# Assembling fp64 weights by clamp, shift, sign merge and integer addition; attention reads in two column tiles; state loads on two queues

## The chip, the cores and the metric

One core of a Trainium2 chip. The metric is the device time of one execution in microseconds (us), lower is better. Engines: PE = TensorE, PEld = its weight loads, DVE = VectorE, ACT = ScalarE, POOL = GpSimd, SP = SyncE. The profiler also records the clock that PE was granted, as a share of full speed; "half clock" below is 0.50 of it.

## The reference

A block-recurrent cross attention, then a gated MLP. The weights come as fp64, the rest as fp32.

```python
# x: (8, 8, 512, 64), state: (8, 8, 32, 64); w_in: (512, 2048), w_out: (2048, 512)
s1 = softmax(x @ state.T / 8);  xread = s1 @ state        # tokens read the states
s2 = softmax(state @ x.T / 8);  sread = s2 @ x            # states read the tokens ("reads")
h = reshape(concat([xread, sread])) @ w_in                # (4352, 512) @ (512, 2048)
out = (h * cos(h)) @ w_out
```

## The kernel before

The batch elements follow each other. For each, the attention is cut into small pieces that stand between the big matmuls of the MLP: `hidden(t)` (weights times attention, into `h`), a gate on ACT and DVE, and `output(t)`. There are 16 slots `t` per batch element. In the first one the weights, which come as pairs of 32-bit words, are also turned into fp32, one chunk per slot, `conv = 3 + t`. All small pieces share one PSUM tile, `at`.

```python
def states():                         # both halves, before the scores
    for half in range(2):
        ...                           # 4 transposes into at[:, half]
        nc.scalar.activation(stS[:, dst], src, func=ACTF.Copy, scale=scale)
        nc.vector.tensor_scalar(stT[:, dst], src, 1.0 / TWO_PI, None, op0=ALU.mult)

def convert1(i):                      # cut: raw, dst, hi, e
    nc.vector.tensor_scalar(e, hi, 0x7FF00000, None, op0=ALU.bitwise_and)       # exponent
    nc.vector.tensor_scalar(dst.bitcast(I32), hi, 0xFFFFF, None, op0=ALU.bitwise_and)
    nc.scalar.activation(e, e, func=ACTF.Relu, bias=ebias, scale=8.0)
    nc.scalar.activation(raw_lo_f32, raw_lo_u32, func=ACTF.Copy, scale=2.0**-52, bias=1.0)
def convert2(i):
    nc.vector.scalar_tensor_tensor(out=e, in0=hi, scalar=-2**31, in1=e, ...)    # sign
    nc.vector.scalar_tensor_tensor(out=dst, in0=dst, scalar=2.0**-20, in1=raw_lo_f32, ...)
def convert3(i):
    nc.vector.tensor_tensor(dst, dst, e.bitcast(F32), op=ALU.mult)

def reads(self, j):
    for c in range(NC):               # 4 matmuls of 256 columns (each is two on PE)
        nc.tensor.matmul(out=at[:, 0, cols], lhsT=self.a2T[:, j, c, :], rhs=..., ...)

for t in tiles(b):                    # one slot
    hidden(t)
    if conv and t.f: convert1(conv + 1); convert2(conv)
    gate(t); gate2(t)                 # ACT copy, DVE
    if conv: convert3(conv)           # cut: the first slot does two chunks
    gate3(t)                          # ACT: Abs, Sin
    go(); ...; output(...)            # go(): one small piece
    gate4(t)                          # DVE
    go()
```

Of the kernel before, what the change touches and what calls it, by code (L numbers as in the profile page):

```python
# [9 lines left out]
F32 = mybir.dt.float32  # L10
I32 = mybir.dt.int32
U32 = mybir.dt.uint32
ALU = mybir.AluOpType
ACTF = mybir.ActivationFunctionType
# [5 lines left out]
TWO_PI = 2.0 * math.pi  # L20
# [3 lines left out]
def kernel(  # L24
# [8 lines left out]
    nc = tc.nc  # L33

    B, H, S, D = x.shape
    Ns = state.shape[2]
    Dm, Dff = moe_w_in.shape
    P = 128
    NK = Dm // P
    NF = Dff // P  # L40
    NC = S // P
    T = S + Ns
    WC = 512
    scale = 1.0 / math.sqrt(D)

    consts = ctx.enter_context(tc.tile_pool(name="consts", bufs=1))
    wraw = ctx.enter_context(tc.tile_pool(name="wraw", bufs=3))
    cvt = ctx.enter_context(tc.tile_pool(name="cvt", bufs=2))
# [14 lines left out]

    halfpi = consts.tile([P, 1], F32)
    nc.vector.memset(halfpi, math.pi / 2.0)
    ebias = consts.tile([P, 1], F32)
    nc.vector.memset(ebias, -896.0 * 2.0 ** 23)




    st = consts.tile([P, B, 2 * D], F32)
    stT = consts.tile([P, B, P], F32)
    stS = consts.tile([P, B, P], F32)
    ident = consts.tile([P, P], F32)
# [4 lines left out]
    def load_x(b):  # L80

        x_b = xin.tile([P, NC, H, D], F32, name="x_b")
        src = x[b].rearrange("h (c p) d -> c p h d", p=P)
        for c in range(NC):
            nc.sync.dma_start(out=x_b[:, c], in_=src[c])
        x_t[b] = x_b
# [2 lines left out]
    st_src = state.rearrange("b (k j) n d -> j k n b d", j=2)  # L89
    for k in range(NK):  # L90
        for j in range(2):
            nc.scalar.dma_start(
                out=st[Ns * k:Ns * k + Ns, :, D * j:D * j + D],
                in_=st_src[j, k])


    at = aps.tile([P, 2, S], F32, name="at")

    def states():
        for half in range(2):  # L100
            for i in range(4):
                nc.tensor.transpose(out=at[:, half, P * i:P * i + P],
                                    in_=st[:, 4 * half + i, :], identity=ident)
            dst = slice(4 * half, 4 * half + 4)
            src = at[:, half].rearrange("p (b m) -> p b m", b=4)
            nc.scalar.activation(stS[:, dst], src, func=ACTF.Copy, scale=scale)
            nc.vector.tensor_scalar(stT[:, dst], src, 1.0 / TWO_PI, None,
                                    op0=ALU.mult)

    w_in = consts.tile([P, NK, Dff], F32)  # L110
    w_out = consts.tile([P, NF, Dm], F32)
# [8 lines left out]
    def in_load(c0, c1, k):  # L120
        return w_in[:, k:k + 2, c0:c1], w_in_src[:, k:k + 2, c0:c1]

    def out_load(f):
# [3 lines left out]
    loads = [in_load(HC * i, HC * i + HC, k) for i in range(2)  # L127
             for k in range(0, NK, 2)]
# [10 lines left out]
    def fetch(n):  # L139
        nonlocal n_fetched  # L140
        while n_fetched < min(n, len(loads)):
            dst, src = loads[n_fetched]
            if f64:
                raw = wraw.tile([P, 2, WC, 2], I32, name="raw")
                raw = raw[:, :, 0:dst.shape[2]]
                nc.sync.dma_start(out=raw.rearrange("p m f w -> p m (f w)"),
                                  in_=src.bitcast(I32))
                raws[n_fetched] = raw
            else:
                nc.sync.dma_start(out=dst, in_=src)  # L150
            n_fetched += 1

    half = {}
# [1 line left out]



    def convert1(i):
        if not f64 or i >= len(loads):
            return  # L160
        raw = raws.pop(i)
        dst = loads[i][0]
        hi = raw[:, :, :, 1]
        e = cvt.tile([P, 2, WC], I32, name="e")[:, :, 0:dst.shape[2]]
        nc.vector.tensor_scalar(e, hi, 0x7FF00000, None, op0=ALU.bitwise_and)  # L165
        nc.vector.tensor_scalar(dst.bitcast(I32), hi, 0xFFFFF, None,
                                op0=ALU.bitwise_and)
        nc.scalar.activation(e, e, func=ACTF.Relu, bias=ebias, scale=8.0)  # L168
        nc.scalar.activation(raw.bitcast(F32)[:, :, :, 0],
                             raw.bitcast(U32)[:, :, :, 0], func=ACTF.Copy,  # L170
                             scale=2.0 ** -52, bias=1.0)
        half[i] = raw, e

    def convert2(i):
        if i not in half:
            return
        raw, e = half[i]
        dst = loads[i][0]
        nc.vector.scalar_tensor_tensor(out=e, in0=raw[:, :, :, 1],  # L179
                                       scalar=-2 ** 31, in1=e,  # L180
                                       op0=ALU.bitwise_and, op1=ALU.bitwise_or)
        nc.vector.scalar_tensor_tensor(out=dst, in0=dst.bitcast(I32),  # L182
                                       scalar=2.0 ** -20,
                                       in1=raw.bitcast(F32)[:, :, :, 0],
                                       op0=ALU.mult, op1=ALU.add)

    def convert3(i):
        if i not in half:
            return
        raw, e = half.pop(i)  # L190
        dst = loads[i][0]
        nc.vector.tensor_tensor(dst, dst, e.bitcast(F32), op=ALU.mult)
        fetch(i + 4)


# [4 lines left out]
    class Attention:  # L200
# [30 lines left out]
        def all_tokens(self):  # L231

            xp = [ops.tile([P, Dm], F32, name="o") for k in range(NK)]
            for c in range(NC):
                for k in range(NK):
                    self.turn_x(k, c, xp[k])
            for k in range(NK):
                if k % 2 == 0:
                    nc.scalar.copy(self.xT[:, k], xp[k])
                else:  # L240
                    nc.vector.tensor_copy(self.xT[:, k], xp[k])
# [73 lines left out]



        def reads(self, j):
            cols = slice(NK * D * j, NK * D * j + NK * D)
            for c in range(NC):  # L320
                nc.tensor.matmul(  # L321
                    out=at[:, 0, cols], lhsT=self.a2T[:, j, c, :],
                    rhs=self.x_b[:, c].rearrange("p (k j) d -> p j k d",
                                                 j=2)[:, j],
                    start=(c == 0), stop=(c == NC - 1))

        def keep(self):
            self.inverse(self.i2)
            src = at[:, 0].rearrange("p (j k d) -> p j k d", j=2, k=NK)
            for k in range(NK):  # L330
                rows = slice(Ns * k, Ns * k + Ns)
                nc.vector.tensor_tensor(
                    self.sr[rows], src[rows, :, k, :],
                    self.i2[rows].unsqueeze(2).to_broadcast([Ns, 2, D]),
                    op=ALU.mult)

# [67 lines left out]
    def gate3(t):  # L404
        nc.scalar.activation(t.q, t.q, func=ACTF.Abs)  # L405
        nc.scalar.activation(t.q, t.q, func=ACTF.Sin, bias=halfpi,  # L406
                             scale=-TWO_PI)
# [53 lines left out]
    fetch(3)  # L461
    a0 = attn[0] = Attention(0)
    a0.all_tokens()
    states()
    a0.scores()
    convert1(0)
    a0.max1()
    a0.spread1()
    a0.shift()
    a0.exp1()  # L470
    convert2(0)
    convert3(0)
    a0.sums()
    convert1(1)
    a0.spread1()
# [3 lines left out]
    a0.first_products(HC)  # L479
    a0.max2()  # L480
    a0.exp2()
    load_x(1)
    convert1(2)
    convert1(3)


# [13 lines left out]
    for b in range(B + 1):  # L500
        work = parts(b + 1) if b + 1 < B else []
        if b == 1:
            work = P1[1:] + work
        n_slots, slot, n_done = 2 * NF, 0, 0

        def go():
            nonlocal n_done, slot
            if b == 0:
                for part in slots0[slot]:
                    part()  # L510
            slot += 1
            want = (len(work) * slot + n_slots - 1) // n_slots
            while n_done < want and b > 0:
                work[n_done]()
                n_done += 1

        for t in tiles(b):
            if t.f == NF // 2 and b + 2 < B:
                load_x(b + 2)
            conv = 3 + t.f if b == 0 else None  # L520
            hidden(t)
            if conv and t.f:
                convert1(conv + 1)
                convert2(conv)
            gate(t)
            gate2(t)
            if conv:
                if t.f == 0:
                    convert2(conv - 1)
                    convert3(conv - 1)  # L530
                    convert2(conv)
                convert3(conv)
            gate3(t)
            go()
            line.append(t)
            if len(line) > 4:
                output(line.pop(0))
            gate4(t)
            if conv and t.f == 0:
                convert1(conv + 1)  # L540
            go()
    for t in line:
        output(t)

# [1 line left out]
_INS = ['x', 'state', 'moe_w_in', 'moe_w_out']  # L546
_OUTS = [((4352, 512), 'float32')]
# [25 lines left out]
```

## Time and profile before

| | before |
|---|---|
| median of the first runs | 892.11 us (891.3 to 893.52) |
| profiled execution | 891.4 us |
| PE, DVE, ACT busy | 93%, 39%, 47% of it |

These shares are averages over three stages with different limits. The lines shown in the prediction below separate them: a chain of latencies to 35 us, the conversion to 147 us, and then PE without a pause. The busy time of one engine in each stretch is what to read.

How much a piece between two big matmuls costs is read from the chain: the next matmul's start, and whether the next ones are longer than usual.

### The profile page before, as it was taken

How to read it: one execution, taken by the hardware profiler on the slowest of the kernel's cores; microseconds unless marked ns; L12 is line 12 of the kernel's file. 1: busy time of each engine (PE TensorE's matmuls, PEld its weight loads, DVE VectorE, ACT ScalarE, POOL GpSimd, SP SyncE). 2: the span in 40 equal slices, each digit the busy share in tenths (PEclk: the TensorE clock that was granted, in tenths of full speed). 3: DMA queues.
4: the chain of work that ended last, by engine and by line, in shares of the span. 5: the costliest groups of instructions: out<-in, count | busy, mean ns of one | idle time of the engine just before them, and what ended most of it. 6: DMA issues, size and time to landing. Idle time of an engine off the chain costs nothing.

```text
span 891.4 us, 7090 instructions
## 1 busy us (share of the span) xinstructions
PE 833.2 (93%) x2720; PEld 382.2 (43%) x2720; DVE 346.3 (39%) x504; ACT 417.8 (47%) x648; POOL 0.7 (0%) x6
## 2 busy tenths in 40 slices
PE   3369968999999999999999999999999999999997
PEld 2025324344444453445344544444344534445664
DVE  1888986234313431352224422442235222222121
ACT  2476574446344634463446434553446344433332
POOL 0000000000000000000000000000000000000000
PEclk9979989999999999999999999999999999999999
DMA  6555620030001200030003000300010000000100
GB/s 141 143 173 179 188 96 1 1 95 1 0 1 57 38 0 1 1 95 1 0 1 95 0 1 0 95 0 1 1 47 1 0 1 24 24 0 1 47 1 24
DMA packets 45377, 35.05 MB, mean 39 GB/s; under 512 B 36384, under 2 KB 36384, under 8 KB 45344
## 3 DMA queue, kind: packets, MB, share of 16 engines
q1 hardware_dynamic: 43168, 34.08, 13.5%
q10 hardware_dynamic: 2176, 0.52, 0.3%
q8 instruction: 21, 0.34, 0.2%
q14 instruction: 12, 0.10, 0.0%
HBM read 25.69 MB, written 8.91 MB: 39 GB/s over the span
## 4 chain that ended last, share of the span: by engine, by line
PE 85%; DVE 7%; ACT 4%; DMA 2%; issue 1%; ACTq 0%; DVEq 0%
PE o L421 49%; PE h L391 26%; PE at L248 4%; PE at L321 3%; DMA st<-in_state_dram 1%; PE at L222 1%; DVE e L179 1%; DVE q L400 1%; PE at L310 1%; ACT q L406 1%; DVE w_out L182 1%; ACT q L405 1%; DVE e L165 1%; DVE w_in L182 1%; ACT e L168 1%
## 5 line engine op out<-in xcount | busy, mean ns | idle before, releaser
L421 PE MATMUL o<-w_out,g 128*128 128x512 f32 x1088 | 492.3, 595 | 0.0
L421 PEld LDWEIGHTS o<-w_out,g 128*128 128x128 f32 x1088 | 203.4, 190 | 244.5 <-issue 240.9
L391 PE MATMUL h<-aT,sw 128*128 128x512 f32 x512 | 249.6, 611 | 2.5 <-ACT sw L353 2.0
L400 DVE SCALAR_TENSOR_TENSOR q<-q,h 128x512 f32<-128x512 f32 (+1 forms) x144 | 94.4, 656 | 338.3 <-ACT q L397 338.2
L397 ACT ACTIVATE q<-h 128x512 f32<-128x512 f32 (+1 forms) x144 | 82.4, 573 | 239.5 <-PE h L391 239.5
L411 DVE TENSOR_TENSOR g<-h,q 128x512 f32<-128x512 f32 (+1 forms) x144 | 95.3, 662 | 161.9 <-ACT q L406 161.9
L391 PEld LDWEIGHTS h<-aT,sw 128*128 128x128 f32 x512 | 95.8, 194 | 121.0 <-issue 107.2
L405 ACT ACTIVATE q<-q 128x512 f32<-128x512 f32 (+1 forms) x144 | 87.3, 606 | 114.5 <-DVE q L400 114.5
L406 ACT ACTIVATE q<-q,halfpi 128x512 f32<-128x512 f32 (+1 forms) x144 | 100.5, 698 | 4.5
L248 PE MATMUL at<-w_in,stT 64*32 64x512 f32 (+1 forms) x512 | 36.8, 616 | 13.7 <-ACT z L287 6.6
L353 ACT COPY sw<-at 128x1024 f32<-128x1024 f32 (+1 forms) x32 | 31.6, 987 | 24.9 <-PE at L248 24.9
L321 PE MATMUL at<-x_b,a2T 128*128 128x256 f32 x128 | 30.6, 382 | 0.0
L391 PE MATMUL h<-sT,w_in 128*128 128x256 f32 x128 | 30.2, 379 | 0.0
L321 PEld LDWEIGHTS at<-x_b,a2T 128*128 128x128 f32 x128 | 24.7, 193 | 10.8 <-issue 8.0
L168 ACT ACTIVATE e<-e,ebias 128x1024 int32<-128x1024 int32 (+1 forms) x18 | 19.0, 1054 | 22.0 <-DVE e L165 22.0
L427 ACT ACTIVATE ot<-o 128x512 f32<-128x512 f32 x34 | 19.3, 591 | 20.8 <-DMA out_dram<-ot 14.1
L391 PEld LDWEIGHTS h<-sT,w_in 128*128 128x128 f32 x128 | 24.3, 190 | 10.1 <-issue 5.3
L222 PEld LDWEIGHTS at<-ident,x_b 128*128 128x128 f32 x112 | 14.7, 148 | 21.8 <-issue 12.6
L222 PE MATMUL at<-ident,x_b 128*128 128x128 f32 x112 | 18.0, 286 | 6.2 <-ACT xT L229 6.2
L248 PEld LDWEIGHTS at<-w_in,stT 64*32 64x32 f32 x512 | 6.1, 106 | 39.8 <-issue 17.6
L229 ACT COPY xT<-at 128x512 f32<-128x512 f32 x28 | 16.0, 573 | 10.1 <-PE at L222 10.1
L179 DVE SCALAR_TENSOR_TENSOR e<-raw,e 128x1024 int32<-128x1024 int32 (+1 forms) x18 | 19.8, 1100 | 0.0
(52 smaller groups left out, 272.5 us busy)
## 6 DMA issues: line engine op xcount, KB each, us to landing
x_b<-in_x_dram SPq DMA_DIRECT2D x32, 256.0 KB, 4.7
raw<-in_moe_w_out_dram SPq DMA_DIRECT2D x8, 1024.0 KB, 4.9
out_dram<-ot SPq DMA_DIRECT2D x32, 256.0 KB, 2.1
raw<-in_moe_w_in_dram SPq DMA_DIRECT2D x6, 1024.0 KB, 5.3
raw<-in_moe_w_in_dram SPq DMA_DIRECT2D x4, 512.0 KB, 6.9
st<-in_state_dram ACTq DMA_DIRECT2D x8, 64.0 KB, 4.9
out_dram<-ot SPq DMA_DIRECT2D x8, 64.0 KB, 1.7
```

Source lines behind the costliest of these rows:

```text
L179: nc.vector.scalar_tensor_tensor(out=e, in0=raw[:, :, :, 1], scalar=-2 ** 31, in1=e, op0=ALU.bitwise_and, op1=ALU.bitwise_or)
L222: nc.tensor.transpose(out=out[:, P * c:P * c + P], in_=self.x_b[:, c, 2 * k:2 * k + 2, :], identity=ident)
L248: nc.tensor.matmul(out=(to[j] if to else at[:, j])[Ns * k:Ns * k + Ns, 0:n], lhsT=w[D * j:D * j + D, self.b, Ns * k:Ns * k + Ns], rhs=r(sl ...
L321: nc.tensor.matmul(out=at[:, 0, cols], lhsT=self.a2T[:, j, c, :], rhs=self.x_b[:, c].rearrange("p (k j) d -> p j k d", j=2)[:, j], start=( ...
L353: nc.scalar.copy(sw_of[self.b, nt][:, :, c0:c1], at[:, :, 0:c1 - c0])
L391: nc.tensor.matmul(out=t.hp, lhsT=t.lhs(i), rhs=t.rhs(i), start=(i == 0), stop=(i == t.kn - 1))
L397: nc.scalar.activation(t.q, t.hp, func=ACTF.Copy, bias=MAGIC)
L400: nc.vector.scalar_tensor_tensor(out=t.q, in0=t.q, scalar=MAGIC, in1=t.hp, op0=ALU.subtract, op1=ALU.subtract)
L405: nc.scalar.activation(t.q, t.q, func=ACTF.Abs)
L406: nc.scalar.activation(t.q, t.q, func=ACTF.Sin, bias=halfpi, scale=-TWO_PI)
L411: nc.vector.tensor_tensor(t.g[:, 0:t.n], t.hp, t.q, op=ALU.mult)
L421: nc.tensor.matmul(out=acc[i], lhsT=t.g[:, P * i:P * i + P], rhs=w_out[:, t.f, :], start=(t.f == 0), stop=(t.f == NF - 1))
```

## The change

The intent is a conversion with four DVE operations per chunk instead of five, reads that use the array as two tiles of 64 columns side by side, and an earlier start. ACT now begins the conversion (`convert0`), and its two passes stand between the gate and `gate3`. The diff is cut.

```diff
-            nc.scalar.dma_start(
+            queue = nc.scalar if j == 0 else nc.gpsimd
+            queue.dma_start(
...
-    def convert1(i):   # two ANDs on DVE, Relu and Copy on ACT
+    def convert0(i):
+        nc.scalar.activation(dst, raw.bitcast(F32)[:, :, :, 1], func=ACTF.Abs)
+        nc.scalar.activation(e, raw.bitcast(U32)[:, :, :, 0], func=ACTF.Copy,
+                             scale=2.0 ** -51, bias=2.0)
+    def convert1(i):
+        nc.vector.tensor_scalar(dst, dst, 2.0 ** -15, None, op0=ALU.max)
+        nc.vector.tensor_scalar(dst.bitcast(I32), dst.bitcast(I32), 3, None,
+                                op0=ALU.logical_shift_left)
     def convert2(i):
+        nc.vector.scalar_tensor_tensor(out=dst, in0=raw[:, :, :, 1],
+                                       scalar=-2 ** 31, in1=dst,
+                                       op0=ALU.bitwise_and, op1=ALU.bitwise_xor)
     def convert3(i):
-        nc.vector.tensor_tensor(dst, dst, e.bitcast(F32), op=ALU.mult)
+        nc.vector.tensor_tensor(dst, dst, e.bitcast(I32), op=ALU.add)
...
-            for c in range(NC):          # x transposes of the first batch element
-                for k in range(NK):
+            for k in range(NK):
+                for c in range(NC):
                     self.turn_x(k, c, xp[k])
...
         def reads(self, j):
+                for k in range(0, NK, 2):
+                    rows = slice(Ns * k, Ns * k + 2 * Ns)
+                    nc.tensor.matmul(
+                        out=at[rows, 0, cols], lhsT=self.a2T[:, j, c, rows],
+                        rhs=x_c[:, j, k:k + 2], start=(c == 0),
+                        stop=(c == NC - 1), tile_position=(0, Ns * k))
...
-    states()
+    states(0)
     a0.scores()
...
     a0.exp2()
+    convert0(2)
+    convert1(2)
+    states(1)
...
             if conv and t.f:
-                convert1(conv + 1)
+                convert1(conv)
                 convert2(conv)
             gate(t)
             gate2(t)
...
                 convert3(conv)
+                convert0(conv + 1)
             gate3(t)
```

More of the change, by code (lines that the diff above doesn't have):

```diff
@@ L65 @@
     nc.vector.memset(halfpi, math.pi / 2.0)
-    ebias = consts.tile([P, 1], F32)
-    nc.vector.memset(ebias, -896.0 * 2.0 ** 23)
     st = consts.tile([P, B, 2 * D], F32)
@@ L97, with states @@
     at = aps.tile([P, 2, S], F32, name="at")
-    def states():
-        for half in range(2):
-            for i in range(4):
-                nc.tensor.transpose(out=at[:, half, P * i:P * i + P],
-                                    in_=st[:, 4 * half + i, :], identity=ident)
-            dst = slice(4 * half, 4 * half + 4)
-            src = at[:, half].rearrange("p (b m) -> p b m", b=4)
-            nc.scalar.activation(stS[:, dst], src, func=ACTF.Copy, scale=scale)
-            nc.vector.tensor_scalar(stT[:, dst], src, 1.0 / TWO_PI, None,
-                                    op0=ALU.mult)
+    def states(half):
+        for i in range(4):
+            nc.tensor.transpose(out=at[:, half, P * i:P * i + P],
+                                in_=st[:, 4 * half + i, :], identity=ident)
+        dst = slice(4 * half, 4 * half + 4)
+        src = at[:, half].rearrange("p (b m) -> p b m", b=4)
+        nc.scalar.activation(stS[:, dst], src, func=ACTF.Copy, scale=scale)
+        nc.vector.tensor_scalar(stT[:, dst], src, 1.0 / TWO_PI, None,
+                                op0=ALU.mult)
     w_in = consts.tile([P, NK, Dff], F32)
@@ L162, in convert1 @@
         dst = loads[i][0]
-        hi = raw[:, :, :, 1]
-        e = cvt.tile([P, 2, WC], I32, name="e")[:, :, 0:dst.shape[2]]
-        nc.vector.tensor_scalar(e, hi, 0x7FF00000, None, op0=ALU.bitwise_and)
-        nc.vector.tensor_scalar(dst.bitcast(I32), hi, 0xFFFFF, None,
-                                op0=ALU.bitwise_and)
-        nc.scalar.activation(e, e, func=ACTF.Relu, bias=ebias, scale=8.0)
-        nc.scalar.activation(raw.bitcast(F32)[:, :, :, 0],
-                             raw.bitcast(U32)[:, :, :, 0], func=ACTF.Copy,
-                             scale=2.0 ** -52, bias=1.0)
-        half[i] = raw, e
+        n = dst.shape[2]
+        e = cvt.tile([P, 2 * WC], F32, name="e")[:, 0:2 * n]
+        e = e.rearrange("p (m f) -> p m f", m=2)
+        nc.scalar.activation(dst, raw.bitcast(F32)[:, :, :, 1], func=ACTF.Abs)
+        nc.scalar.activation(e, raw.bitcast(U32)[:, :, :, 0], func=ACTF.Copy,
+                             scale=2.0 ** -51, bias=2.0)
+        half[i] = raw, e
+    def convert1(i):
+        if i not in half:
+            return
+        dst = loads[i][0]
+        nc.vector.tensor_scalar(dst, dst, 2.0 ** -15, None, op0=ALU.max)
+        nc.vector.tensor_scalar(dst.bitcast(I32), dst.bitcast(I32), 3, None,
+                                op0=ALU.logical_shift_left)
     def convert2(i):
@@ L177, in convert2 @@
         raw, e = half[i]
-        dst = loads[i][0]
-        nc.vector.scalar_tensor_tensor(out=e, in0=raw[:, :, :, 1],
-                                       scalar=-2 ** 31, in1=e,
-                                       op0=ALU.bitwise_and, op1=ALU.bitwise_or)
-        nc.vector.scalar_tensor_tensor(out=dst, in0=dst.bitcast(I32),
-                                       scalar=2.0 ** -20,
-                                       in1=raw.bitcast(F32)[:, :, :, 0],
-                                       op0=ALU.mult, op1=ALU.add)
+        dst = loads[i][0].bitcast(I32)
+        nc.vector.scalar_tensor_tensor(out=dst, in0=raw[:, :, :, 1],
+                                       scalar=-2 ** 31, in1=dst,
+                                       op0=ALU.bitwise_and,
+                                       op1=ALU.bitwise_xor)
     def convert3(i):
@@ L190, in convert3 @@
         raw, e = half.pop(i)
-        dst = loads[i][0]
-        nc.vector.tensor_tensor(dst, dst, e.bitcast(F32), op=ALU.mult)
+        dst = loads[i][0].bitcast(I32)
+        nc.vector.tensor_tensor(dst, dst, e.bitcast(I32), op=ALU.add)
         fetch(i + 4)
@@ L233, in all_tokens @@
             xp = [ops.tile([P, Dm], F32, name="o") for k in range(NK)]
-            for c in range(NC):
-                for k in range(NK):
+            for k in range(NK):
+                for c in range(NC):
                     self.turn_x(k, c, xp[k])
-            for k in range(NK):
                 if k % 2 == 0:
@@ L318, in reads @@
         def reads(self, j):
-            cols = slice(NK * D * j, NK * D * j + NK * D)
+            cols = slice(2 * D * j, 2 * D * j + 2 * D)
             for c in range(NC):
-                nc.tensor.matmul(
-                    out=at[:, 0, cols], lhsT=self.a2T[:, j, c, :],
-                    rhs=self.x_b[:, c].rearrange("p (k j) d -> p j k d",
-                                                 j=2)[:, j],
-                    start=(c == 0), stop=(c == NC - 1))
+                x_c = self.x_b[:, c].rearrange("p (k j) d -> p j k d", j=2)
+                for k in range(0, NK, 2):
[4 more added lines that the diff above has]
+                        stop=(c == NC - 1), tile_position=(0, Ns * k))
         def keep(self):
             self.inverse(self.i2)
-            src = at[:, 0].rearrange("p (j k d) -> p j k d", j=2, k=NK)
+            src = at[:, 0, 0:4 * D].rearrange("p (j k d) -> p j k d", j=2,
+                                              k=2)
             for k in range(NK):
@@ L332, in keep @@
                 nc.vector.tensor_tensor(
-                    self.sr[rows], src[rows, :, k, :],
+                    self.sr[rows], src[rows, :, k % 2, :],
                     self.i2[rows].unsqueeze(2).to_broadcast([Ns, 2, D]),
@@ L463 @@
     a0.all_tokens()
-    states()
+    states(0)
     a0.scores()
+    convert0(0)
     convert1(0)
@@ L472 @@
     convert3(0)
+    convert0(1)
     a0.sums()
@@ L481 @@
     a0.exp2()
+    convert0(2)
+    convert1(2)
+    states(1)
     load_x(1)
-    convert1(2)
+    convert0(3)
     convert1(3)
@@ L538 @@
             gate4(t)
-            if conv and t.f == 0:
-                convert1(conv + 1)
             go()
```

## The prediction

> **What bounds the kernel now.** I read the engine totals first, then busy time by stage, then the chain of work that ended last, then the groups by shape, then single stretches of the timeline.
>
> The stage table splits the run in three (columns: stretch, its length, busy us and instruction counts of PE, PEld, DVE, ACT, POOL, then granted clock, DMA share, GB/s):
>
> ```profile
> 0.00:35.00 35.00, 11.21 (x57) 5.41 (x58) 16.44 (x25) 7.83 (x12) 0.70 (x6) 1.00 0.50 117
> 35.00:147.00 112.00, 85.05 (x285) 36.37 (x285) 97.08 (x123) 74.92 (x100) 0.00 (x0) 0.90 0.48 147
> 147.00:891.00 744.00, 736.95 (x2380) 340.38 (x2378) 232.76 (x357) 335.02 (x536) 0.00 (x0) 1.00 0.07 20
> ```
>
> To 35 us no engine is full: it is a chain of latencies. From 35 to 147 the weights are converted and DVE is busy 97.1 of 112 us (87%). From 147 on PE is busy 737 of 744 us, so only work taken off PE counts there. The change touches all three stages, each by another rule.
>
> The chain at the start (start us, us, what) shows the latencies:
>
> ```profile
> 2.53 4.64 DMA st<-in_state_dram
> 7.19 7.37 DMA st<-in_state_dram
> ...
> 14.69 1.10 PE at L102 x4
> ...
> 15.81 0.60 ACT stS L106
> ...
> 16.44 0.70 DVE stT L107
> ...
> 17.19 1.13 PE at L102 x4
> ...
> 19.72 2.04 PE at L248 x16
> ```
>
> The states land at 14.55 us; the fifth load left only when an earlier one had landed (7.19). Then two rounds of transposes, ACT, DVE stand before the scores at 19.72.
>
> The groups of the conversion (the 1024-wide forms, up to 220 us) are what DVE does in the middle stage:
>
> ```profile
> L179 DVE SCALAR_TENSOR_TENSOR e<-raw,e 128x1024 int32<-128x1024 int32 x14 | 17.1, 1221 | 0.0
> L192 DVE TENSOR_TENSOR w_out<-w_out,e 128x1024 f32<-128x1024 f32 x8 | 9.8, 1221 | 0.0
> L165 DVE TENSOR_SCALAR e<-raw 128x1024 int32<-128x1024 int32 x14 | 9.5, 677 | 1.1 <-DMA raw<-in_moe_w_in_dram 1.1
> L166 DVE TENSOR_SCALAR w_out<-raw 128x1024 int32<-128x1024 int32 x8 | 5.5, 687 | 0.0
> ```
>
> Neighbours overlap a little: in the timeline they start 0.60 us (one input) and 1.13 us (two inputs) apart. Where one needs the result of the one just before, the start comes about 0.03 us after its end, so 0.71 us.
>
> The chain in the last stage gives the price of the reads (L321) and of leaving the full array shape (L248 works in tiles of 64x32):
>
> ```profile
> 410.27 1.72 PE h L391 x4
> 411.99 1.73 PE at L321 x8
> 413.72 3.43 PE o L421 x8
> ...
> 431.19 1.02 PE at L248 x16
> 432.21 3.63 PE o L421 x8
> ```
>
> One reads step is 8 matmuls of 256 columns, 0.216 us each. L421 takes 3.43 us after the reads but 3.63 after L248.
>
> **What the Trainium skill says.** (1) "VectorE: DVE Perf Modes", The perf-mode tier table: an fp32 tensor_scalar in SBUF runs at twice the rate of a tensor_tensor. The trace agrees: 0.68 against 1.22 us for 1024 elements, for bit operations on int32 too. So max and shift should cost 0.68, sign merge and integer addition 1.22. (2) "TensorEngine Tiling (Array Packing)", Key Properties: different tiles can load weights and multiply in parallel, and changing the tiling mode drains TensorE. The trace agrees: 16 tiled matmuls of 512 columns, 0.427 us each if alone, take 1.02 us, and about 0.2 is lost after them. (3) "TensorE: Matmul & The Clock Gate", Part 1: the array runs at half clock until it has been busy for about 3.4 us. In this trace the same transpose takes 0.417 us at the start and 0.272 later. (4) "DMA: Bandwidth & Descriptors", SWDGE vs HWDGE vs iDMA: a GpSimd DMA has its descriptors built by software. The built program shows the four POOL loads as that kind; no run so far shows their time.
>
> **The change part by part.**
>
> *Start.* Four state loads per queue instead of eight on one: none needs to wait for an earlier landing. The states should land near 9 to 11 us instead of 14.55 (estimate: 1.5 MB of x and states at the 181 GB/s of the first 10 us is 8.7 us, from about 1.9 us). But the order of the 16 x transposes is turned: the first four now need all four x chunks, so all 16 run after the last chunk, at 9.58. Four took 1.11 us with the tail of the last, about 0.23 each, so 16 end at 13.3. Before, only four were left then. So PE, not the state load, holds the next step: transposes of half the states 13.3 to 14.4, ACT 0.6, DVE 0.7, scores near 15.75 instead of 19.72: 4.0 us gained, 2.5 of it by moving the second half of the states away.
>
> *First two half chunks.* On the softmax chain each loses one 0.60 us operation: 1.2 us. Second maximum done at 30.0 instead of 35.2.
>
> *Second half of the states.* It now stands after the second exponential and ahead of the first hidden matmul on PE. That exponential ends near 31.5, the transposes at 32.5, and the hidden matmul at half clock (3.6 us) at 36.2. The first gate was at 38.89: the gain shrinks to 2.7.
>
> *Slot 0.* Two half chunks follow; 1.2 us less on DVE, and the ACT work for two full chunks no longer stands ahead of the second gate. It was at 49.91 while its matmul had ended near 48.7; I get 44.6: gain 5.3.
>
> *Slots 1 to 4.* Here the change costs. ACT now does the two conversion passes (1.05 + 1.05 us, 2.15) between the gate and its Abs, where it used to wait 0.75 for DVE. Abs and Sin (1.36), the PSUM copy (0.5 to 1.0), the next PE piece, which waits for that copy because both use the tile at, and the hidden matmul follow in a chain: 0.6 + 2.15 + 1.36 + 0.5 + 1.1 + 3.43 + 0.2 = 9.3 us in a slot at half clock (7.85 before), about 7.5 with two such pieces at full clock, 5.6 where there is none. Gates 1 to 5 took 27.6 us; 9.3 + 7.6 + 7.4 + 5.6 = 29.9. Given back: 2.3.
>
> *Slots 5 to 14.* A full chunk was 0.60 + 0.60 + 1.13 + 1.13 + 1.13 = 4.59 us of DVE; it becomes 0.71 + 0.71 + 1.13 + 1.13 = 3.68, the first two now depending on each other: 0.91 less. Nine slots held 9 x (4.59 + 1.3 of gates) + 12 of attention = 65 us of DVE in 70.0 us (gate 77.50 to 147.55). After: 9 x 4.98 + 12 = 57 us of DVE, and PE needs 9 x (1.72 + 3.43) + about 12 = 58. Two engines at that level that wait for each other do not reach it; at nine tenths it is 64.2 us: 5.8 gained.
>
> So the PE-bound stage begins 5.3 - 2.3 + 5.8 = 8.8 us earlier.
>
> *Reads.* 16 steps, 14 of them in the PE-bound stage. Eight matmuls of 128 columns per tile at 0.107 to 0.125 us are 0.86 to 1.0, both tiles at once, plus the mode switch: the 64x32 pieces cost 1.02 + 0.2 against 0.853 of data, 0.36. Together 1.3 instead of 1.73: 0.43 x 14 = 6.0 us.
>
> Sum: 892.1 - 8.8 - 6.0 = 877.3; I say 877.
>
> **The rivals.** *DVE sets the middle stage alone:* then 14 x 1.13 + 4 x 0.6 = 18 us come off, the start gives 4, the reads 6: 864. For it: DVE at 87%. Against it: PE had 85 of those 112 us, and ACT's new order lengthens the chain. *The new ACT order takes the bound:* with slots near 7.5 us throughout, the middle gains little: 892 - 3 - 6 = 883. Against it: in slots 5 to 14 half the pieces need no copy. *The tiles do not overlap, or their weight loads show:* then a reads step costs 1.73 + 0.36, 14 x 0.36 = 5 us lost: 888. Against it: the 64x32 tiles do overlap, and transposes with 128-column loads follow each other at 0.11 us. *Slow POOL loads:* hidden until 13.3 us; each us later costs one. *The half clock:* PE stood at half clock in two windows after 110 us and several before 60; which matmuls fall into them can move 2 us either way.
>
> **Range and chances.** About 3 us of uncertainty at the start and in the slots, 2 in the clock, 2 in the reads: 867 to 884. Two per cent faster is 874.3, inside the range on the good side: 0.33 faster, 0.66 same, 0.01 slower.
>
> **What would show it.** Scores at about 15.7 us, held by x transposes and not by a state load; gate 1 near 44.6 and gate 5 near 74.5; ACT's conversion passes between gate and Abs, with PE waiting for a copy of at; DVE no longer above 85% in the middle; the stage with full PE from about 139; reads steps of 1.2 to 1.4 us, counting what the next matmuls lose. I am wrong if reads steps are not shorter than 1.73, if integer additions take clearly over 1.22 us, or if POOL's loads land after 14 us.

## The result

| | before | after |
|---|---|---|
| median | 892.55 us (891.3 to 893.52, 4 runs) | 880.0 us (879.0 to 880.86, 4 runs) |
| profiled execution | 891.4 us | 877.2 us |
| ratio | | 0.986, 95% interval 0.9843 to 0.9877 |

A ratio is the mean time of one kernel's fast runs over that of the other's of the same rounds, so it is not quite the ratio of the medians. The change is 1.4% faster, clear of noise and within the 2% band.

The stage table of the changed kernel, columns as in the prediction:

```profile
0.00:35.00 35.00, 12.53 (x60) 6.56 (x60) 17.29 (x26) 11.30 (x21) 3.13 (x10) 0.76 0.68 164
35.00:147.00 112.00, 90.14 (x339) 38.94 (x340) 83.44 (x105) 72.24 (x95) 0.00 (x0) 0.88 0.41 132
147.00:877.00 730.00, 722.75 (x2450) 326.23 (x2449) 230.07 (x354) 332.98 (x533) 0.00 (x0) 1.00 0.07 20
```

Between 35 and 147 us DVE fell from 97 to 83 of 112 us, and PE rose from 85 to 90, in part because the last stage now begins before 147 (gate 14, below, is at 140.72). DVE is no longer the busiest engine there. The clock column of the first stage can't be compared: it reads 1.00 up to the first recorded step of the clock, which before the change came near 42 us, though the scores at 19.72 took 1.96 us, against the 1.09 us that they took after it.

Its start, from the chain that ended last:

```profile
3.14 7.17 DMA x_b<-in_x_dram
...
10.35 3.03 PE o L223 x13
13.39 0.76 PE at L99 x4
...
14.17 0.61 ACT stS L103
...
14.80 0.70 DVE stT L104
...
15.55 1.17 PE at L248 x16
```

No state load is left in it. The last x chunk holds PE to 10.35 us, and 13 of the 16 transposes stand behind it; the first three could go earlier. The scores start at 15.55 us (19.72 before).

The DVE groups of the new conversion (1024-wide chunks of `w_out`, up to 220 us):

```profile
L183 DVE SCALAR_TENSOR_TENSOR w_out<-raw,w_out 128x1024 int32<-128x1024 int32 x8 | 9.8, 1225 | 0.3
L193 DVE CUSTOM_DVE_ANT_0 w_out<-w_out,e 128x2048 uint16<-128x2048 uint16 x8 | 9.7, 1218 | 0.0
L175 DVE TENSOR_SCALAR w_out<-w_out 128x1024 int32<-128x1024 int32 x8 | 5.6, 694 | 0.3
L174 DVE TENSOR_SCALAR w_out<-w_out 128x1024 f32<-128x1024 f32 x8 | 5.4, 671 | 0.0
```

The integer addition is a custom operation over 16-bit halves, twice as many elements. It still costs 1.22 us, as the fp32 multiplication did.

The chain in the last stage:

```profile
400.17 1.72 PE h L395 x4
401.88 1.02 PE at L325 x16
402.91 3.63 PE o L425 x8
```

A reads step takes 1.02 us instead of 1.73, and the matmuls behind it 3.63 instead of 3.43: the price of a tile mode, as after L248.

To see where the time went, I use five marks of each profiled execution: the start of the scores, the starts of the ACT gate copies of slots 1, 5 and 14 in the first batch element, and the rest to the end of the span.

| us | scores | gate 1 | gate 1 to 5 | gate 5 to 14 | gate 14 to end | median of runs |
|---|---|---|---|---|---|---|
| before | 19.72 | 49.91 | 27.59 | 70.05 | 743.9 | 892.55 |
| after | 15.55 | 42.75 | 34.21 | 63.76 | 736.5 | 880.0 |
| difference | -4.17 | -7.16 | +6.62 | -6.29 | -7.4 | -12.55 |

The four differences from gate 1 on add up to -14.2 us, which is what the two profiled executions differ by. The medians differ by less because the profiled execution before was a long one (893.29 us as a run) and the one after the shortest of its four (879.0). The surprise is the third column: slots 1 to 4 got 6.6 us longer. ACT in slot 3 of the changed kernel, from its timeline (start us, duration, instruction, and in brackets the idle time before it and what ended it):

```profile
61.20 0.60 ACT L401 ACTIVATE q<-h 128x512 f32<-128x512 f32 x1 [2.83 <-PE h L395]
61.70 1.17 ACT L165 ACTIVATE w_in<-raw 128x1024 f32<-128x1024 f32 x1
62.75 1.13 ACT L166 ACTIVATE e<-raw 128x1024 f32<-128x1024 uint32 x1
63.77 0.63 ACT L409 ACTIVATE q<-q 128x512 f32<-128x512 f32 x1
64.43 0.72 ACT L410 ACTIVATE q<-q,halfpi 128x512 f32<-128x512 f32 x1
65.06 0.99 ACT L357 COPY sw<-at 128x1024 f32<-128x1024 f32 x1
67.26 0.58 ACT L313 COPY a2T<-at 128x512 f32<-128x512 f32 x1 [1.20 <-PE at L310]
70.67 0.60 ACT L401 ACTIVATE q<-h 128x512 f32<-128x512 f32 x1 [2.83 <-PE h L395]
```

The two conversion passes (L165, L166) stand between the gate and the Abs (L409). Then ACT waits twice for PE, which in turn had waited for ACT's copy of `at`. Before, the passes (L168, L169) lay at the end of the slot, where ACT waits for the hidden matmul anyway. The same slot before the change, with the next gate at 71.29 us and no wait in front of it:

```profile
64.31 0.60 ACT L397 ACTIVATE q<-h 128x512 f32<-128x512 f32 x1
65.67 0.63 ACT L405 ACTIVATE q<-q 128x512 f32<-128x512 f32 x1 [0.76 <-DVE q L400]
...
69.18 1.15 ACT L168 ACTIVATE e<-e,ebias 128x1024 int32<-128x1024 int32 x1
70.23 1.18 ACT L169 ACTIVATE raw<-raw 128x1024 f32<-128x1024 uint32 x1
```

The 6.6 us are of two kinds. Between gates 1 and 5 PE was busy 18.28 of 27.59 us before (mean clock 0.88) and 21.69 of 34.21 us after (0.75), with nearly as many instructions (68 and 66): 3.4 us more of busy time at a lower clock, and 3.2 us more of idle time.

### The profile page after: what moved, and what is told of

It is laid out like the page before. It is cut to its first block, busy times and chain, and to the rows that moved or that the text cites. A ratio compares the mean times of both kernels' runs of the same rounds, so it can differ in the third digit from the quotient of the medians.

```text
span 877.2 us, 7341 instructions
## 1 busy us (share of the span) xinstructions
PE 825.4 (94%) x2848; PEld 371.7 (42%) x2848; DVE 330.8 (38%) x485; ACT 416.5 (47%) x648; POOL 3.1 (0%) x10
## 3 DMA queue, kind: packets, MB, share of 16 engines
q10 hardware_dynamic: 1088, 0.26, 0.2%
## 4 chain that ended last, share of the span: by engine, by line
PE 88%; DVE 5%; ACT 5%; DMA 1%; issue 0%; SPq 0%; DVEq 0%; ACTq 0%
PE o L425 51%; PE h L395 28%; PE at L248 4%; PE at L325 2%; PE at L223 1%; PE at L310 1%; ACT q L410 1%; DMA x_b<-in_x_dram 1%; ACT q L409 1%; ACT e L166 1%; DVE q L404 1%; DVE w_in L183 0%; ACT q L401 0%; DVE m L261 0%; DVE w_out L183 0%; DVE spread L267 0%
## 5 line engine op out<-in xcount | busy, mean ns | idle before, releaser
L409 ACT ACTIVATE q<-q 128x512 f32<-128x512 f32 (+1 forms) x144 | 87.2, 606 | 107.6 <-DVE q L404 107.5
L248 PE MATMUL at<-w_in,stT 64*32 64x512 f32 (+1 forms) x512 | 37.0, 620 | 8.4 <-ACT z L287 4.7
L248 PEld LDWEIGHTS at<-w_in,stT 64*32 64x32 f32 x512 | 6.1, 107 | 34.8 <-issue 12.9
L267 DVE STREAM_TRANSPOSE spread<-m 128x1024 f32<-128x1024 f32 x16 | 19.8, 1235 | 0.0
L166 ACT ACTIVATE e<-raw 128x1024 f32<-128x1024 uint32 (+1 forms) x18 | 18.8, 1044 | 0.0
L325 PEld LDWEIGHTS at<-x_b,a2T 128*64 128x64 f32 x256 | 13.6, 136 | 12.1 <-issue 10.6
L325 PE MATMUL at<-x_b,a2T 128*64 128x128 f32 x256 | 17.5, 279 | 0.0
```

The source lines that it names most:

```text
L166: nc.scalar.activation(e, raw.bitcast(U32)[:, :, :, 0], func=ACTF.Copy, scale=2.0 ** -51, bias=2.0)
L248: nc.tensor.matmul(out=(to[j] if to else at[:, j])[Ns * k:Ns * k + Ns, 0:n], lhsT=w[D * j:D * j + D, self.b, Ns * k:Ns * k + Ns], rhs=r(sl ...
L325: nc.tensor.matmul(out=at[rows, 0, cols], lhsT=self.a2T[:, j, c, rows], rhs=x_c[:, j, k:k + 2], start=(c == 0), stop=(c == NC - 1), tile_p ...
L409: nc.scalar.activation(t.q, t.q, func=ACTF.Abs)
```

## The experiments

My theory after the result: the reads cost PE time and count wherever PE is the bound; the conversion frees DVE, but ACT's new order gives much of it back in slots 1 to 4, partly because PE then idles so much that its clock stays at half. The rivals: the reads are hidden; DVE alone sets the middle stage; slots 1 to 4 are long by chance of the clock.

### The reads alone

The kernel before with only the new `reads` (and `keep`, which takes their result).

> The kernel before with only the reads in two tiles of 64 columns. Theory (reads cost PE time, which is the bound from 147 us on): a reads step takes 1.02 us and the matmuls behind it lose 0.2, so 0.51 us less per step than 1.73; 14 steps in the PE-bound stage give 7.1 us, and the two steps of the first batch, where PE also had no slack at 75 to 84 us, up to 1 us more: 884 to 886 us. Rival (the gain of the whole change comes from the conversion, the reads are hidden): within 2 us of before, 890 to 893.

Measured: 884.77 us, ratio 0.9916 (0.99 to 0.9932). Gate 14 to the end fell from 743.9 to 736.4 us, 7.4 us, while nothing else became faster. The theory holds; the reads are the larger half of the whole gain.

### The changed kernel with the old reads

> The changed kernel with the reads put back to one tile of 128 columns. Theory: the mirror image of the reads alone, 880 + 7 to 8 = 887 to 888 us, about 0.5 to 0.6% faster than before. Rival (parts do not add, because PE work only shows where PE is the bound): clearly less than 5 us lost, 885 or below.

Measured: 887.21 us, ratio 0.9941 (0.9927 to 0.9955), and gate 14 to the end back at 743.6 us. The part adds to the others within the noise: 7.2 us lost here, 7.9 gained alone.

### The arithmetic alone

The kernel before with the new conversion and its place in ACT's order, without the other three parts.

> The kernel before with only the new arithmetic of the weights and its place in ACT's order; state loads on one queue, x transposes by chunk, both halves of the states first, old reads. Theory (DVE loses 0.91 us per chunk but ACT's two passes now stand between gate and Abs and cost that back in slots 1 to 4): scores stay near 19.7 us, gate 0 near 36 to 37, gate 14 near 143 to 145 instead of 147.5, total 887 to 890. Rival (DVE alone sets the stage to 147 us): 18 us of DVE come off and the total is 874 to 877.

Measured: 889.78 us, ratio 0.9968 (0.9953 to 0.9982). Gate 1 came 3.2 us earlier (46.75), slots 1 to 4 took 32.93 us (5.3 more than before), slots 5 to 14 took 64.79 (5.3 less). The rival with 18 us of DVE taken off the total is refuted: DVE's busy time fell by 15.5 us (346.3 to 330.8), the profiled execution by 3.1. By the medians this part is worth 2.9 us and the reads 7.9, which leaves about 2 of the 12.6 us for the start; this remainder was not run by itself.

### ACT's second pass at the end of the slot

```diff
                 convert3(conv)
-                convert0(conv + 1)            # both passes
+                convert0(conv + 1, now=False) # Abs of the high words only
             gate3(t)
 ...
             gate4(t)
             go()
+            if conv:
+                convert0b(conv + 1)           # the low words
```

> The changed kernel, but of ACT's two conversion passes only the first (Abs of the high words) stands between gate and Abs; the second (low words) is done at the end of the slot, where ACT waits for the hidden matmul. Theory (ACT's order lengthens the chain of slots 1 to 4): 1.05 us off the chain of each of four slots and a PE that idles less, gates 1 to 5 in about 29 us instead of 34.2, and 875 to 877 us in total. Rival (the slots are long only because the clock was at half by chance): gates 1 to 5 stay near 34 us and the total within 1.5 us of 880.

Measured: 874.06 us, ratio 0.9786 (0.977 to 0.9803). Slots 1 to 4 took 26.80 us instead of 34.21, a larger gain than the expected one (to about 29). Slot 3 on ACT:

```profile
58.43 0.60 ACT L408 ACTIVATE q<-h 128x512 f32<-128x512 f32 x1 [1.24 <-PE h L402]
58.92 1.14 ACT L165 ACTIVATE w_in<-raw 128x1024 f32<-128x1024 f32 x1
59.96 0.62 ACT L416 ACTIVATE q<-q 128x512 f32<-128x512 f32 x1
...
62.98 0.58 ACT L320 COPY a2T<-at 128x512 f32<-128x512 f32 x1 [0.75 <-PE at L317]
63.46 1.18 ACT L174 ACTIVATE e<-raw 128x1024 f32<-128x1024 uint32 x1
64.70 0.60 ACT L408 ACTIVATE q<-h 128x512 f32<-128x512 f32 x1
```

The second pass (L174) now lies where ACT had waited 2.83 us for the hidden matmul, and the next gate follows it without a wait. The slot took 6.27 us instead of 9.47. So ACT's order is a cause. The gain exceeds one pass per slot; the mean clock of these slots was also higher, 0.86 instead of 0.75, and the next experiment takes the clock by itself.

### Filler matmuls

```diff
             gate3(t)
             go()
+            if b == 0 and 1 <= t.f <= 3:      # two matmuls nobody reads
+                spare = ops.tile([P, Dm], F32, name="o")
+                for _ in range(2):
+                    nc.tensor.matmul(out=spare, lhsT=ident, rhs=stS[...], start=True, stop=True)
```

> The changed kernel with two useless matmuls (128x512, results never read) in each of slots 1 to 3, behind the first PE piece, where PE waits for ACT. The question is how much of the slots' length is the half clock by itself. Theory A (half clock is the larger part: each hidden matmul group takes 3.4 instead of 1.7 us): with PE kept busy the clock stays full, gates 1 to 5 fall from 34.2 to about 28 to 29 us and the total to 874 to 876. Theory B (the length of ACT's chain is it; the clock hardly matters): gates 1 to 5 stay within 2 us of 34 and the total within 2 us of 880.

Measured: 878.09 us in the median, but from 873.22 to 879.41; ratio 0.9813 (0.9786 to 0.9839). The profiled run was one of the two short ones, 873.59. The stretch from gate 1 to gate 5, changed kernel first, then this one (PE's clock is the figure after the engines' busy times, before DMA share and GB/s):

```profile
42.75:76.96 34.21, 21.69 (x66) 10.33 (x68) 21.95 (x28) 19.84 (x29) 0.00 (x0) 0.75 0.42 141
```

```profile
43.63:70.33 26.70, 20.35 (x78) 9.20 (x78) 20.22 (x25) 19.78 (x27) 0.00 (x0) 0.99 0.51 167
```

With 12 more matmul instructions PE was busy for less time, at a clock of 0.99 instead of 0.75: the hidden matmuls of slots 1 to 3 took 1.88 us each, against 3.0 to 3.6 in the changed kernel. The slots took 26.70 us with ACT's order untouched, less than the 27.59 before the change. So in this execution the loss went away with the half clock alone, as theory A has it; the late pass had taken back as much by ACT's order. Read together, ACT's order makes PE idle and the idling brings the half clock about; that chain is argued from these two runs, one trace each, and not shown step by step.

The median, though, is theory B's (within 2 us of 880): four of the six runs were at 877.6 to 879.4 us. I have no trace of those. Their mean clock over the whole run (0.987 to 0.991) was not lower than that of the two short ones (0.983, 0.984), but that mean counts everything before the first recorded step as full clock and settles nothing. What kept them long stays open.

### Both passes at the end of the slot

> The changed kernel with both conversion passes of ACT at the end of the slot. Theory (what counts is both ACT's chain and that DVE has its input early): slots 1 to 4 stay as short as with one pass late (26.8 us for gates 1 to 5), but DVE gets its input only some 2 us later, so slots 5 to 14 lengthen by several us against 63.4: total 876 to 880. Rival (only the passes between gate and Abs cost): another 1 us per slot gained, total 870 to 872.

Measured: 878.51 us, ratio 0.9833 (0.9814 to 0.9852). Slots 1 to 4 took 28.76 us, but slots 5 to 14 took 66.77 instead of 63.76. Who waited for whom on DVE between gates 5 and 14 (us in total, times, longest):

```profile
DVE w_out L174 <- ACT w_out L165: 4.0, 3, 3.1
...
DVE w_in L174 <- ACT w_in L165: 2.3, 2, 1.9
```

DVE now waits 6.3 us for the first pass, a wait that is not among those of the changed kernel's same slots. Slots 1 to 4 did not get as short as the 26.8 us expected. The two passes have different readers: the first is needed early in the next slot, the second only by its last DVE operation. Each belongs in another gap.

### The x transposes chunk by chunk

The changed kernel with the old loop order of the first transposes.

> The changed kernel with the x transposes in their old order, chunk by chunk. In the changed kernel the states had landed by 8.4 us and the last x chunk at 10.3; 13 transposes then took 3.0 us. Theory: only four are left after the last chunk, the scores start 1.0 to 1.6 us earlier than 15.55, and as PE then is at half clock there they take 1.96 instead of 1.09 us, so 0.3 to 1 us is left: 879 to 880 us. Rival (the start's gain passes through whole): 878 or less.

Measured: 877.63 us (877.56 to 878.37), ratio 0.9823 (0.9803 to 0.9843). The scores start at 14.10 us, and no run overlaps those of the changed kernel, though the intervals of the ratios do. About 2 us are gained. That is the rival's answer (878 or less), not the theory's (879 to 880): beside the changed kernel's repeat (below), whose scores also ran at half clock, the scores came 1.75 us earlier and gate 1 came 1.80 us earlier, so the start's gain passed through whole. The new order of the transposes was a loss in itself.

### Both halves of the states first

> The changed kernel with both halves of the states turned before the scores, as before the change. Theory: scores 2.5 us later (18.0 instead of 15.55), but the first hidden matmul no longer stands behind the second half's transposes (1.1 us), so gate 0 comes about 1.3 us later and the total is 881 to 882. Rival (the start counts whole): 882.5 or more.

Measured: 880.54 us, ratio 0.9854 (0.9833 to 0.9874): no difference from the changed kernel, so this expectation was too pessimistic. The scores came 2.6 us later than in the repeat (18.44), but the first hidden matmul did not. PE of this kernel, then of the changed kernel's repeat (next part):

```profile
32.40 3.78 PE L395 MATMUL h<-aT,sw 128*128 128x512 f32 x4 [0.48 <-ACT sw L365]
```

```profile
32.00 1.12 PE L99 MATMUL at<-ident,st 128*128 128x128 f32 x4 [2.67 <-ACT z L287]
32.91 3.45 PE L395 MATMUL h<-aT,sw 128*128 128x512 f32 x4
```

Where the second half stands after the scores, its transposes wait for the second exponential (which reads `at`) and the hidden matmul waits behind them in PE's order. That takes back all of what the move had gained.

### The changed kernel again, and one queue for the states

> The changed kernel itself, unchanged, so that the versions beside it have it on the same chip: 879 to 881 us, ratio to before 0.985 to 0.987. If it differs by more than 2 us from 880, differences of that size between calls mean nothing.

Measured: 879.69 us, ratio 0.9836 (0.9818 to 0.9855), the same time as in the first rounds, on another chip. (The ratio was put at 0.985 to 0.987; it is lower because the kernel before took 894.01 us in these rounds.) Its profiled execution had other clock windows: the scores were at 15.85 and at half clock, gate 1 at 45.25, slots 1 to 4 took 33.34 us, slots 5 to 14 took 63.75. So single marks up to gate 1 carry some 2.5 us of clock phase; the long slots 1 to 4 were no accident of one execution.

> The changed kernel with all eight state loads on ACT's queue. Theory: the loads 5 to 8 again wait for earlier landings, the states land near 14 to 14.5 us instead of 8.4, about 1 us after PE is ready for them (13.4), so the scores start 1 to 1.5 us later and the total is 881 to 882. Rival 1 (PE hides it): 880. Rival 2 (x lands earlier, because fewer state packets compete with it, and the 16 transposes with it): scores at 15.5 or earlier, total 879 to 880.

Measured: 880.99 us, ratio 0.9853 (0.9834 to 0.9872). On one queue the state transposes waited 2.69 us for a load and the scores started at 16.96, 1.1 us later than the repeat beside it; but gate 14 was at 142.52 against 142.34. The expected wait is there; in the total the second queue is worth 1.3 us or nothing, the intervals overlap.

### Better versions

> A better version: the changed kernel with ACT's second pass at the end of the slot (gained 6 us) and the x transposes by chunk (gained 2.4 us). If both gains add: 871 to 872.5 us, ratio to before 0.975 to 0.977. If the phase of the clock decides what the earlier start is worth: 873 to 875.

Measured: 872.25 us, ratio 0.9756 (0.9737 to 0.9776). The second pass at the end of the slot and the transposes by chunk add up, within the noise.

> The same with the useless matmuls in slots 1 to 3 as well. With one pass late the slots are already short of ACT work, so PE idles less; what is left is the half clock in two or three windows. If the clock stays full: another 2 to 3 us, 868.5 to 870. If its windows fall as they like: a spread of several us between runs, as the fillers alone had (873 to 879), and no gain in the median.

Measured: 870.49 us (869.75 to 871.51), ratio 0.9739 (0.9721 to 0.9757), the fastest of all: 1% under the changed kernel's repeat of the same rounds. The slots 1 to 4 took 25.93 us. Against the version without fillers the intervals overlap; here the fillers did not spread the runs. In the profiled executions gate 14 came 3.1 us earlier than without fillers, the end only 1.3.

All profiled marks, for comparison:

| us | scores | gate 1 | gate 1 to 5 | gate 5 to 14 | gate 14 to end | median |
|---|---|---|---|---|---|---|
| reads alone | 20.29 | 50.50 | 28.20 | 70.77 | 736.4 | 884.77 |
| old reads | 15.77 | 42.90 | 34.16 | 64.77 | 743.6 | 887.21 |
| arithmetic alone | 20.05 | 46.75 | 32.93 | 64.79 | 743.8 | 889.78 |
| second pass late | 15.40 | 43.49 | 26.80 | 63.37 | 736.3 | 874.06 |
| fillers | 15.51 | 43.63 | 26.70 | 63.75 | 737.7 | 878.09 |
| both passes late | 15.93 | 45.45 | 28.76 | 66.77 | 735.3 | 878.51 |
| chunk order | 14.10 | 43.45 | 32.09 | 63.75 | 736.5 | 877.63 |
| states together | 18.44 | 45.71 | 33.31 | 63.77 | 736.8 | 880.54 |
| changed again | 15.85 | 45.25 | 33.34 | 63.75 | 736.5 | 879.69 |
| one queue | 16.96 | 45.83 | 32.95 | 63.74 | 736.5 | 880.99 |
| late and chunk | 14.11 | 43.56 | 27.66 | 63.34 | 736.4 | 872.25 |
| late, chunk, fillers | 14.03 | 42.18 | 25.93 | 63.33 | 738.3 | 870.49 |

## Why the prediction was right

877 us was predicted, 867 to 884 as the range; 880.0 was measured. Point by point:

- **Start.** Scores near 15.75 us, held by x transposes and not by a state load: 15.55 and 15.85, with the x chunk and 13 transposes in the chain. Right, in part by luck: the last chunk let PE go on at 10.35 us, not at the 9.58 of before, but 13 transposes were left then and not 16. That the second half of the states gives its gain back at the first hidden matmul was in the prediction too; the run with both halves first confirms it.
- **Up to gate 1.** 5.3 us predicted, 7.2 and 4.7 us in the two profiled executions. Right within the clock's phase.
- **Slots 1 to 4.** The sign and the mechanism were right, the size was not: 2.3 us given back were predicted, 6.6 and 5.8 measured. The mis-sized term is the sum 9.3 + 7.6 + 7.4 + 5.6: slots 2 to 4 were put at full clock. The slots took 9.46, 8.99, 9.47 and 6.29 us. The clock stood at half in most of them; with fillers, at 0.99, they took 6.9, 6.9, 7.3 and 5.6. So gate 5 came at 76.96 and 78.59, not near 74.5.
- **Slots 5 to 14.** 64.2 us predicted, 63.76 measured, by the estimate that two engines near 57 us of work that wait for each other reach nine tenths. The trace has PE busy 57.6 us and DVE 55.4: 0.90 of the stretch for the busier one, as DVE was 0.89 of it before (62.4 of 70.05). The prediction assumed that share and did not derive it.
- **Reads.** 1.3 us per step and 6.0 in all predicted; 1.22 and 7.4 measured. The mode switch cost what it costs in the other tiled pieces.
- **Sum.** For the profiled executions 8.8 + 6.0 = 14.8 was predicted and 14.2 measured: the loss in slots 1 to 4 was put 4.3 too small, and the gains elsewhere 3.7 too small. The middle of the estimate is partly a cancellation.
- **Slips that did not matter.** The load that left at 7.19 us was the eighth, not the fifth, which left at 4.39. Turning the order leaves 13 transposes behind the last chunk, not all 16. Two passes of 1.05 us are 2.10, not 2.15; the trace has 2.07.

The rival of DVE setting the middle stage alone (864) is refuted by the arithmetic alone; the rival of ACT's order (883) was the nearer one for slots 1 to 4, and wrong for 5 to 14.

## What to carry to other kernels

When work is taken off the busiest engine, look at where its remaining inputs are made: a pass placed in front of a short wait on another engine can lengthen the one chain that matters, while the same pass in a longer wait costs nothing. Give each half of such work the latest gap that its own reader allows. And a PE that waits in the middle of a pipeline can pay twice, by the wait and by a lower clock after it: here 3.2 us of idle time came with 3.4 us more of busy time.

## What the Trainium skill lacked or had wrong

- "VectorE: DVE Perf Modes", Specifications: it says that integer operands are converted and exact only below 2^24, and no page gives the price of a full int32 addition on this engine. Here it ran as a custom operation over 16-bit halves, with a correct result, at 1.22 us for 1024 words per partition, as much as an fp32 tensor_tensor.
- "TensorEngine Tiling (Array Packing)", Key Properties: it names the drain at a mode switch without a size. Here a reads step cost 1.02 + 0.2 us; one tile's eight matmuls of 128 columns, at half the 0.216 us that 256 columns took, are 0.86 us, so by this estimate, which takes the two tiles to run at the same time throughout, entering and leaving the mode cost about 0.36 us.
- "TensorE: Matmul & The Clock Gate", Part 4: it says that transposes do not engage the full clock. In the changed kernel's profiled execution PE did nothing but transposes up to 14.2 us (one PE record each, where an fp32 matmul has two), and the scores at 15.55 us ran at full rate (1.09 us; 1.96 in the repeat, at half).
- The same page, Part 1: it speaks of busy and idle windows and does not say what share of work in them keeps the clock up. Here PE was busy 21.7 of 34.2 us and had a mean clock of 0.75; two more matmuls in each of three slots brought 0.99, with 20.35 of 26.70 us busy, in the one execution traced.
- "DMA: Bandwidth & Descriptors" gives times for GpSimd loads to 128 partitions, none for loads of 64 KB to 32 partitions in rows of 256 bytes beside other traffic. Here four of them landed in 5.7 us each (median), in 128 packets altogether, against 4.4 us and 1088 packets for the four on ACT's queue.
